# Fused attention and gated MLP on one NeuronCore: where the scale products and the token-mixing bias of two batches are computed, and when eight weight blocks are stored

## The chip, the cores and the metric

One core of a Trainium2 chip runs the whole program. The metric is the device time of one execution in microseconds (us); the time given for a kernel is the median of its runs. The engines are named as the profile names them: PE (TensorE's matmuls), PEld (its weight loads), DVE (VectorE), ACT (ScalarE), POOL (GpSimd) and SP (SyncE, which here only issues DMAs). Each engine executes its own instructions in the order in which the kernel writes them.

## What is computed

Grouped-query attention over 8 batches (16 query heads, 4 key heads, 384 tokens, head size 64) gives `x` of 384 x 1024 per batch. Then comes a block that mixes tokens and channels:

```python
a1 = alpha1 * x + beta1
tok = np.einsum('ts,bsd->btd', w_tok, a1)
u = x + lam * tok
a2 = alpha2 * u + beta2
ch = np.maximum(a2 @ w_ch1, 0.0) @ w_ch2
return (u + lam * ch).astype(np.float32)
```

`w_ch1` is 1024 x 4096, `w_ch2` 4096 x 1024; inputs and output are float32, the products are made in bfloat16.

## The kernel before

**Pairs, phases, steps.** The batches go through the MLP in four pairs (`pair(ps)`, ps = 0 to 3). A pair has phase 0, the product with `w_ch1`, and phase 1, the product with `w_ch2`. Both are made from blocks of the weights in seven products instead of eight, so sums and differences of weight blocks are needed too. `pair` is a generator that yields after every small group of matmuls; each yield is a *step*. In pair 0, phase 0 has 100 steps in eight groups, and phase 1 has 84: 21 turns `(o, ms)` of 16 matmuls, four steps a turn, so turn k ends with step 4k+3. The dictionary `plan` says by hand what is emitted after step (pair, phase, step): `put(0, 1, 41, keep_w2, 1, 0)` emits that call after step 41 of phase 1 of pair 0.

**Attention beside phase 1.** While pair 0 is in phase 1, the attention and token mixing of batches 2 and 3 are emitted between its steps (`side(2)` from step 0, `side(3)` from step 38 on). They go by eight head pairs p:

- `scores3` makes scores on PE, and ACT takes their exponentials (L269);
- `av` (`av_piece`) multiplies by the values on PE (L295); then DVE normalizes (L300, L303) and makes `a1` in bfloat16, the operand of the token mixing;
- `tok` multiplies `a1` by the token weights on PE (L324), DVE adds `x` (L331) and multiplies by alpha2 (L334); SP stores u (`spill`, L227) and, for batch 2, turns a2 by a DMA transpose (L337);
- for batch 3 `turn` turns a2 on PE (L398), and ACT copies it out (L400).

All PSUM tiles of this attention come from `three()`, which hands out three double banks in rotation. `g1` holds alpha1 * lam and `h1` holds beta1 * lam, so that lam * tok comes out of the product directly.

**The fold.** For `fold` batches (0 to 3) `av_piece` makes `a1` with one product (L309), and the bias enters in `tok` by an extra matmul per output block, R against H (L328): R is made of the row sums of the token weights and H of beta1 * lam. H and R lie in the memory of `h1`. Other batches do without that matmul and make `a1` with two DVE operations, a product and an addition (L312, L313). In pair 1, `h1` is filled: `rows4_on` clears two row tiles on POOL and loads beta1 with two SP DMAs, `to_all` spreads it over the partitions on DVE (L1037), `scale_beta` multiplies it by lam on DVE (L1040).

**The second product of pair 0.** `second_product` ends a turn by an ACT copy (L764) and for o = 6 and 7 a DVE addition (L767). Finished output tiles (128 x 512) are queued in `later` and handled by `flush`, which calls `scaled`: a product with lam (L790), on POOL if `lead` (pair 0) and otherwise on DVE, and then an accumulating store (L442), a DMA that POOL issues. In phase 1 of pair 0 nine such tiles are flushed, after the fourth or twelfth matmul of a turn: for steps 12, 16 and 28, and for steps 68, 70, 72, 74, 76 and 78. The last three are flushed in phase 0 of pair 1.

**W2's blocks.** `w_ch2` is cut into blocks "11", "12", "21", "22" with four parts c each. `load_w2` loads them; `sum_w2` overwrites them by sums on DVE (L499). Raw blocks and sums are stored in DRAM tiles `w2s` (`keep_w2`, an SP DMA of 512 KB each), from where later pairs fetch them. Part c of "11" is overwritten by `sum_w2(7, c)` after steps 51, 54, 57 and 58, which has to wait until its store has read it; the slots of "22" are freed by PE in steps 44 to 47. The slots `w` are a ring of six; `pump` gives free ones to the next loads, which POOL issues ("again" blocks: SP).

**Order on the queues.** Instructions of a step are emitted as: matmuls of the step, the end of a turn, a flush, then the plan's entries in the order of their `put`.

Of the kernel before, what the change touches and what calls it, by code (L numbers as in the profile page):

```python
# [13 lines left out]
def kernel(  # L14
# [21 lines left out]
    nc = tc.nc  # L36
# [4 lines left out]
    MUL = mybir.AluOpType.mult  # L41
# [43 lines left out]
    g1, h1, al2, lam_t = (vecs[:, i] for i in range(4))  # L85
# [10 lines left out]
    turn, a2_turn = [0], [0]  # L96
# [117 lines left out]
    def side(b):  # L214
        vb = vt[b % 2]
        ess, avs, a1s, a2s, xr = {}, {}, {}, {}, {}
        first, fold = b < 2, b < 4
        kT_, qT_ = kTs.get(b, kT), qTs.get(b, qT)

        def x_of(p):  # L220
# [170 lines left out]
        def by_pe(p):  # L391
            return b in (0, 3) or b % 2 and p >= NP - (4 if first else 3)
# [14 lines left out]
        def put(k, *m):  # L407
            at.setdefault(k, []).append(m)
# [3 lines left out]
        for p in range(NP):  # L412
            put((4, 10, 14, 18, 24, 29, 33, 35)[p], av, p)
            put((8, 15, 17, 22, 27, 32, 36, 38 if b % 2 else 39)[p], tok_flip, p)
            if by_pe(p):
                put(((13, 20, 22, 28, 34, 37, 40, 42) if b == 3 else (0, 0, 0, 0, 0, 36, 39, 41))[p], turn, p)
        return at

    def loads(b):
# [21 lines left out]
    def store(b, ms, dw, o):  # L441
        nc.gpsimd.dma_start(out=by_tok(out[b])[:, ms, dw * 512:(dw + 1) * 512], in_=o, accum_op=ADD)  # L442
# [19 lines left out]
    def spare(i):  # L462
        at = 24 * S + i % 3 * 1024
        return hTf[:, at:at + 1024]
# [102 lines left out]
    def free_blocks(side, gp):  # L567
        for kind in (side + "1", side + "2"):
            if (kind, gp) in block_slot:
                free(block_slot.pop((kind, gp)))  # L570
# [201 lines left out]
    def pair(i):  # L772
        b0 = 2 * i
        lead = i == 0
# [12 lines left out]

        def scaled(o, b, ms, dw, t):
            if o != 2 or not last:
                (nc.gpsimd if lead else nc.vector).tensor_tensor(out=t, in0=t, in1=lam_t[:, dw * 512:(dw + 1) * 512], op=MUL)  # L790
            store(b, ms, dw, t)

        def flush(n=9):
# [18 lines left out]
        if lead:  # L812
            yield from first_product(flush)
            share_banks("sc0", "acc", "sc1", "sc2")
            yield from second_product(pairs["acc"], later, flush, scaled)
            return

        for g in range(NH // 2):
            X, Y, snap = {}, {}, {}
            for k, (o, e) in enumerate(SEQ1):  # L820
                t = 2 * g + e
# [54 lines left out]
        for k, o in enumerate(PLACE2):  # L876
            whole = not last and o != 4
            tail = last and o == 4
            for h in range(1 if whole else 2):
                for ms in range(NST - (tail and not h)):  # L880
# [37 lines left out]
                    if (whole or h == 1) and not (last and o == 4):  # L918
                        if o in (1, 6, 5):
                            q = ((1, 6, 5).index(o) * NST + ms) * 512  # L920
                            snap[o, ms] = snaps[:, q:q + 512]
                        else:
                            bb, dw = where[o]
                            t = snap[1, ms] if o == 7 else spare(ms).bitcast(f32)
                        for c0, c1, x in X[ms]:
                            if o == 1:
                                nc.scalar.copy(out=snap[o, ms], in_=x)
                            elif o in (6, 5):
                                tt(out=snap[o, ms], in0=x, in1=snap[1 if last or o == 6 else 6, ms], op=ADD)
                            elif o == 2 and last:  # L930
                                tt(out=t, in0=x, in1=lam_t[:, :512], op=MUL)
                            else:
                                base = {2: 1, 3: 1 if last else 5, 7: 5, 4: 6}[o]
                                tt(out=t[:, c0:c1], in0=x, in1=snap[base, ms][:, c0:c1], op=ADD)
                            if o == 7 and not last:
                                tt(out=snap[6, ms], in0=x, in1=snap[6, ms], op=ADD)
                        if o not in (1, 6, 5):
                            later.append((scaled, o, b0 + bb, ms, dw, t))
# [8 lines left out]
    with tc.manual_schedule(engines=order):  # L947
# [123 lines left out]
        def put(ps, phase, at, *m):  # L1071
            plan.setdefault((ps, phase, at), []).append(m)
# [17 lines left out]
        put(0, 0, 8, rows4_on, (3, 0), (3, 1))  # L1090
        put(0, 0, 30, to_all, 3, 0, 0)
        put(0, 0, 34, to_all, 3, 1, 1)
        put(1, 0, 20, rows4_on, (1, 0), (1, 1))
        put(1, 0, 54, to_all, 1, 0, 0)
        put(1, 0, 68, to_all, 1, 1, 1)
        put(1, 0, 62, scale_beta, 0)
        put(1, 0, 76, scale_beta, 1)
        for c in range(4):
            put(0, 0, (50, 72, 74, 44)[c], load_w2, "11", c)
            put(0, 0, (6, 14, 42, 46)[c], cast_w2, "21", c)  # L1100
            put(0, 1, (41, 43, 45, 47)[c], keep_w2, 1, c)
            put(0, 1, 38 + 2 * c, keep_w2, 3, c)
            put(0, 1, (9, 10, 13, 15)[c], sum_w2, 5, c)
            put(0, 1, (20, 21, 25, 26)[c], sums_first_hid, 2, c)
            put(0, 1, (28, 30, 31, 34)[c], sums_first_hid, 4, c)
            put(0, 1, (37, 40, 41, 43)[c], sum_w2, 6, c)
            put(0, 1, (44, 45, 49, 50)[c], sums_first_hid, 3, c)
            put(0, 1, (51, 54, 57, 58)[c], sum_w2, 7, c)
            put(0, 1, (61, 64, 68, 71)[c], last_w2, c)
        for u, o in ((77, 5), (79, 7), (81, 6)):  # L1110
            put(0, 1, u, sum_w1, 0, o)
        for ps in range(NB - 1):
            c = 2 * ps + 2
            for i in range(9):
                put(ps, 0, (4, 8, 12, 16, 20, 24, 54, 58, 62)[i] if ps == 0 else 4 + 7 * i, load_next, c, 1)
                put(ps, 0, 70 + 3 * i if ps == 0 else 91 + 2 * i, load_next, c + 1, 1)
            put_flips(ps, 0, c, (44, 46, 50, 54, 58) if ps == 0 else range(76, 86, 2))
            put_all(ps, 1, side(c))
            for u, f, h in zip((8, 14, 14, 27, 32, 33) if ps == 0 else (10, 17, 18, 28, 33, 33),
                               (flip_q, flip_k, flip_q, flip_q, flip_k, flip_q), (0, 0, 2, 4, 2, 6)):  # L1120
                put(ps, 1, u, f, c + 1, h, 2)
            put_all(ps, 1, side(c + 1), lambda u: u + 38)
            for j, u in ((0, 77), (2, 80), (3, 83)) if ps == 0 else ((0, 76), (2, 79), (3, 81)):
                put(ps, 1, u, sums_a, j, 1 if j else 2)

        def steps(ps):
            done = [0, 0]
            for second in pair(ps):
                for f, *a in plan.pop((ps, second, done[second]), []):
                    f(*a)  # L1130
                done[second] += 1
                yield
            for key in [k for k in plan if k[0] == ps]:
                for f, *a in plan.pop(key):
                    f(*a)

        first = steps(0)
# [76 lines left out]
```

## Time and profile before

| | us |
|---|---|
| runs of the kernel | 732.49, 732.74, 738.95 (median 732.74) |
| profiled execution, its own time | 731.92 |
| its span, first to last instruction | 729.9 |
| pair 0, phase 0 | about 59 to 129 |
| pair 0, phase 1 (with batches 2 and 3) | about 129 to 234 |
| pairs 1 to 3 | about 234 to 725 |

The profile is of one execution; its own time is 2.0 us longer than its span. A row of groups has the source line, the engine, the operation, output and input, the shape and count, then the busy time in us and the mean of one in ns, then idle time before it. A row of the timeline has the start, the duration, the engine, the line and the instruction, and in brackets the idle time of the engine before it and what ended that.

### The profile page before, as it was taken

Reading aid. Unit: us, or ns where it says so; the run is one execution under the profiler, and the core shown is the slowest. Engines: PE = TensorE matmul, PEld = TensorE weight load, DVE = VectorE, ACT = ScalarE, POOL = GpSimd, SP = SyncE. Lnnn points to the kernel's source line nnn. Section 1 sums busy time; section 2 is a strip of 40 time slices with the busy share of each in tenths; the row PEclk is TensorE's granted clock in tenths of the full one; section 3 lists DMA queues with packets and bytes.
Section 4 is the critical chain, followed back from the end, with each engine's and each line's share of the span. In section 5 each row is a group of like instructions: output and inputs, shape, how many; then the busy total and the mean of one; then the engine's idle time right before and its main releaser. Section 6 shows DMA issues by size and latency. Waiting matters only on the chain.

```text
span 729.9 us, 14511 instructions
## 1 busy us (share of the span) xinstructions
PE 717.4 (98%) x5716; PEld 408.7 (56%) x5716; DVE 543.9 (75%) x1009; ACT 373.8 (51%) x566; POOL 199.2 (27%) x242
## 2 busy tenths in 40 slices
PE   8899999999999999999999999999999999999998
PEld 4665555555555666555555566655555566654444
DVE  7888876577888988649678888748868988763354
ACT  7877666544563666643433466663333366650000
POOL 8844233221046551201022344200002222000011
PEclk9999999999999999999999999999999999999999
DMA  9999999999999999969989999998989999937965
GB/s 164 180 239 231 190 195 227 226 242 235 366 312 232 179 182 196 234 221 207 272 193 220 160 162 194 212 227 201 270 233 183 210 126 146 165 123 264 302 174 104
DMA packets 197616, 153.26 MB, mean 210 GB/s; under 512 B 90540, under 2 KB 175892, under 8 KB 197292
## 3 DMA queue, kind: packets, MB, share of 16 engines
q0 software_dynamic: 109872, 64.47, 65.4%
q1 hardware_dynamic: 86988, 87.42, 42.8%
q8 instruction: 44, 0.72, 0.4%
q10 hardware_dynamic: 688, 0.46, 0.2%
q14 instruction: 24, 0.20, 0.1%
HBM read 155.23 MB, written 39.85 MB: 267 GB/s over the span
## 4 chain that ended last, share of the span: by engine, by line
PE 90%; DVE 4%; POOL 2%; DMA 1%; issue 1%; ACT 1%; DVEq 0%; ACTq 0%; POOLq 0%
PE C L897 30%; PE X L831 17%; PE C L752 10%; PE Y L831 9%; PE Z L831 4%; PE sc L260 4%; PE X L681 4%; PE sc L295 3%; PE sc L324 3%; PE Y L681 3%; DMA ops<-obuf 1%; DVE pad L565 1%; PE Z L681 1%; PE tok L324 1%; POOL obuf L334 0%
## 5 line engine op out<-in xcount | busy, mean ns | idle before, releaser
L897 PE MATMUL C<-w,arena 128*128 128x512 bf16 (+2 forms) x744 | 168.3, 372 | 0.0
L269 ACT ACTIVATE es<-sc 128x1024 bf16<-128x1024 f32 x108 | 104.1, 1024 | 116.0 <-PE sc L260 107.6
L897 PEld LDWEIGHTS <-arena 128*128 128x128 bf16 x1040 | 94.8, 98 | 100.5 <-issue 5.1
L442 POOL DMA_DIRECT2D out_dram<-hT x45 | 40.0, 888 | 294.7 <-DVE hT L790 135.9
L836 ACT ACTIVATE hT<-X,bias 128x384 f32<-128x384 f32 x144 | 83.6, 582 | 60.0 <-PE X L831 55.2
L831 PEld LDWEIGHTS <-w 128*128 128x128 bf16 x768 | 75.1, 98 | 50.0
L831 PEld LDWEIGHTS <-pad 128*128 128x128 bf16 x576 | 56.4, 98 | 37.2
L183 POOL DMA_DIRECT2D w<-in_moe_w_ch_dram x48 | 45.4, 1002 | 105.6 <-PE X L831 36.5
L831 PE MATMUL X<-ops,w 128*128 128x384 bf16 x384 | 70.3, 326 | 0.0
L831 PE MATMUL X<-ops,pad 128*128 128x384 bf16 x384 | 70.3, 326 | 0.0
L897 PE MATMUL C<-pad,arena 128*128 128x512 bf16 (+2 forms) x296 | 70.2, 373 | 0.0
L324 PEld LDWEIGHTS <-wtokT 128*128 128x128 bf16 x576 | 39.0, 98 | 16.4 <-issue 3.4
L752 PEld LDWEIGHTS <-arena 128*128 128x128 bf16 x336 | 29.8, 98 | 30.0 <-issue 2.5
L331 DVE TENSOR_TENSOR xr<-sc,xr 128x384 f32<-128x384 f32 x48 | 26.5, 553 | 25.6 <-PE sc L324 14.3
L752 PE MATMUL C<-w,arena 128*128 128x512 bf16 x168 | 41.2, 379 | 0.0
L838 DVE TENSOR_TENSOR arena<-Y,hT 128x384 bf16<-128x384 f32 x48 | 26.5, 556 | 17.7 <-ACT hT L836 16.0
L295 PEld LDWEIGHTS <-es 128*128 128x128 bf16 x864 | 32.8, 97 | 11.3
L831 PE MATMUL Y<-ops,w 128*128 128x384 bf16 x192 | 39.1, 326 | 0.0
L831 PE MATMUL Z<-ops,w 128*128 128x384 bf16 x192 | 39.0, 326 | 0.0
L269 ACT ACTIVATE hT<-sc 128x1024 bf16<-128x1024 f32 x36 | 35.8, 1031 | 4.3 <-PE sc L260 4.0
L260 PE MATMUL sc<-qT,kT 64*128 64x384 bf16 (+2 forms) x504 | 37.2, 271 | 0.5 <-ACT hT L269 0.2
L842 ACT ACTIVATE arena<-X,bias 128x384 bf16<-128x384 f32 x48 | 27.9, 582 | 17.7 <-PE X L831 16.1
(190 smaller groups left out, 1175.1 us busy)
## 6 DMA issues: line engine op xcount, KB each, us to landing
w<-w2s SPq DMA_DIRECT2D x67, 512.0 KB, 5.1
w<-in_moe_w_ch_dram POOLq DMA_DIRECT2D x65, 512.0 KB, 9.8
pad<-w2s SPq DMA_DIRECT2D x25, 512.0 KB, 6.9
out_dram<-hT POOLq DMA_DIRECT2D x45, 256.0 KB, 7.1
out_dram<-xr SPq DMA_DIRECT2D x48, 192.0 KB, 5.3
q_raw<-in_q_dram POOLq DMA_DIRECT2D x28, 192.0 KB, 9.5
w2s<-w SPq DMA_DIRECT2D x10, 512.0 KB, 7.6
arena<-in_moe_w_ch_dram POOLq DMA_DIRECT2D x8, 512.0 KB, 15.9
```

Of the source, the lines that this page charges most:

```text
L183: nc.gpsimd.dma_start(out=w1[:, w1_slots[c]], in_=w1src[:, :, c * CW * P:(c + 1) * CW * P])
L260: nc.tensor.matmul(out=sc[:, hh, k % 4:k % 4 + n], lhsT=kT_[r, 2 * p // G, BLK[hh][sk], :], rhs=qT_[r, p, st:st + n, :], start=True, stop= ...
L269: nc.scalar.activation(out=e, in_=sc, func=EXP, scale=scale_qk)
L295: nc.tensor.matmul(out=av[:, hh, sq, :], lhsT=ess[k // 4][:, m % 2, k % 4, :], rhs=vb[:, sk, hk, :], start=(sk == 0), stop=(sk == NST - 1))
L324: nc.tensor.matmul(out=ps[:, tt, :], lhsT=wtokT[:, st, tt * P:(tt + 1) * P], rhs=a1s[p][:, st, :], start=(st == 0), stop=(st == NST - 1 an ...
L442: nc.gpsimd.dma_start(out=by_tok(out[b])[:, ms, dw * 512:(dw + 1) * 512], in_=o, accum_op=ADD)
L681: nc.tensor.matmul(out=ps[:, :n], lhsT=tb[G, o][:, dt, e * P:(e + 1) * P], rhs=opb(FIRST1[o], n)[:, dt], start=(o in (1, 2, 7) and dt == 0 ...
L752: nc.tensor.matmul(out=x, lhsT=lead_hid[:, t, FIRST2[o], ms * P:(ms + 1) * P], rhs=rhs[:, t % 4 * 512:(t % 4 + 1) * 512], start=(o in (1, ...
L831: nc.tensor.matmul(out=ps, lhsT=tb[g, o][:, dt, e * P:(e + 1) * P], rhs=opb(LEFT1[o])[:, dt], start=(o in (1, 2, 7) and dt == 0), stop=(dt ...
L836: nc.scalar.activation(out=snap[o, e], in_=ps, func=IDENT, bias=hi if o == 5 else lo)
L842: nc.scalar.activation(out=hid[:, t, 4], in_=ps, func=RELU, bias=hi)
L897: nc.tensor.matmul(out=x, lhsT=hid[:, t, LEFT2[o], ms * P:(ms + 1) * P], rhs=rhs[:, t % 4 * 512 + c0:t % 4 * 512 + c1], start=((not last o ...
```

## The change

Four things are edited, all in what pair 0 does or in what batches 2 and 3 do.

1. Batches 2 and 3 are no longer folded: no L328 matmuls, and `a1` by L312 and L313.
2. For that, `h1` has to be filled before batches 2 and 3: `rows4_on`, `to_all` and `scale_beta` move from phase 0 of pair 1 to phase 0 of pair 0 (steps 40, 54, 59, 64 and 69), when batches 0 and 1 are done with H and R.
3. The lam products of pair 0 go to DVE; POOL still issues the stores.
4. The stores of the raw "11" and "22" go from steps 38 to 47 to steps 16 to 37. Besides, `turn` of p = 2 of batch 3 is emitted one step later (step 61 instead of 60, behind `tok` of p = 3).

```diff
-        first, fold = b < 2, b < 4
+        first = fold = b < 2
...
-                put(((13, 20, 22, 28, 34, 37, 40, 42) if b == 3 else (0, 0, 0, 0, 0, 36, 39, 41))[p], turn, p)
+                put(((13, 20, 23, 28, 34, 37, 40, 42) if b == 3 else (0, 0, 0, 0, 0, 36, 39, 41))[p], turn, p)
...
-                (nc.gpsimd if lead else nc.vector).tensor_tensor(out=t, in0=t, in1=lam_t[:, dw * 512:(dw + 1) * 512], op=MUL)
+                nc.vector.tensor_tensor(out=t, in0=t, in1=lam_t[:, dw * 512:(dw + 1) * 512], op=MUL)
...
-        put(1, 0, 20, rows4_on, (1, 0), (1, 1))
-        put(1, 0, 54, to_all, 1, 0, 0)
-        put(1, 0, 68, to_all, 1, 1, 1)
-        put(1, 0, 62, scale_beta, 0)
-        put(1, 0, 76, scale_beta, 1)
+        put(0, 0, 40, rows4_on, (1, 0), (1, 1))
+        for i in range(2):
+            put(0, 0, 54 + 10 * i, to_all, 1, i, i)
+            put(0, 0, 59 + 10 * i, scale_beta, i)
...
-            put(0, 1, (41, 43, 45, 47)[c], keep_w2, 1, c)
-            put(0, 1, 38 + 2 * c, keep_w2, 3, c)
+            put(0, 1, (16, 18, 20, 22)[c], keep_w2, 1, c)
+            put(0, 1, (24, 32, 34, 37)[c], keep_w2, 3, c)
```

## Prediction

> **What bounds the kernel now.** I read the busy shares first, then the chain of work that ended last, then the stage that is changed in the stretches table, and last the timelines of PE, DVE, POOL and SP there.
>
> ```profile
> PE 717.4 (98%) x5716; PEld 408.7 (56%) x5716; DVE 543.9 (75%) x1009; ACT 373.8 (51%) x566; POOL 199.2 (27%) x242
> ...
> PE 90%; DVE 4%; POOL 2%; DMA 1%; issue 1%; ACT 1%; DVEq 0%; ACTq 0%; POOLq 0%
> ```
>
> PE is busy nearly throughout, at a granted clock of 1.00, and carries 90% of the chain. From 234.5 to 725 the stretches show PE busy without a gap, so whatever pair 0 gains or loses arrives at the end. The change acts in 77 to 235 us. Its stretches (length, then busy time of PE, PEld, DVE, ACT, POOL):
>
> ```profile
> 190.00:200.00 10.00, 10.00 (x106) 5.84 (x105) 8.43 (x13) 5.29 (x8) 0.91 (x1) 1.00 1.00 359
> 200.00:212.00 12.00, 11.41 (x107) 6.29 (x106) 9.95 (x15) 7.33 (x12) 0.96 (x2) 1.00 1.15 333
> 212.00:220.00 8.00, 8.00 (x91) 4.68 (x88) 6.86 (x9) 5.31 (x9) 7.08 (x7) 1.00 1.25 273
> 220.00:228.00 8.00, 6.81 (x72) 4.03 (x69) 7.57 (x10) 3.58 (x7) 7.03 (x7) 1.00 1.17 240
> 228.00:235.00 7.00, 7.00 (x41) 3.47 (x39) 6.86 (x16) 1.97 (x4) 1.60 (x2) 1.00 1.05 240
> ```
>
> PE rests twice: near 204, and between 220 and 228, where DVE is full. The chain in 190 to 236 names the two places (start, duration, what):
>
> ```profile
> 203.81 1.04 ACT es L269
> 204.85 0.04 issue
> 204.89 0.33 PE sc L324 x3
> ...
> 220.87 2.02 DVE w L499
> 222.89 0.11 DVE rinv L300
> 223.00 0.02 issue
> 223.03 0.57 DVE xr L303
> 223.60 0.02 issue
> 223.62 1.09 DVE a L309
> 224.71 0.04 issue
> 224.76 0.34 PE sc L324 x3
> ```
>
> At 204.89 `tok` of p = 3 waits for a PSUM bank that the second exponential releases; at 224.76 `tok` of p = 6 waits for its `a1`. Two durations in that second chain are too long: L499 of this shape takes 1.22 elsewhere, L309 0.56. Both run beside POOL's lam products:
>
> ```profile
> L790 POOL TENSOR_TENSOR hT<-hT,vecs 128x512 f32<-128x512 f32 x12 | 18.6, 1552 | 17.6 <-ACT hT L764 17.6
> L790 DVE TENSOR_TENSOR hT<-hT,vecs 128x512 f32<-128x512 f32 x30 | 20.6, 686 | 0.4
> L309 DVE TENSOR_TENSOR a<-xr,vecs 128x384 bf16<-128x384 f32 x16 | 11.8, 736 | 0.6
> L312 DVE TENSOR_TENSOR a1f<-xr,vecs 128x384 f32<-128x384 f32 x32 | 17.9, 558 | 1.1
> ```
>
> L309 averages 736 ns where the like L312 averages 558. The long ones start while a POOL product runs (L309 at 143.15 takes 1.33, POOL's product lasts from 142.79 to 144.05).
>
> **The change part by part.**
>
> *48 matmuls less.* The chain shows one L328 as 0.06 us, and three L324 as 0.17; 48 x 0.0557 = 2.67 us of PE, in a stage where PE has work. I take -2.67.
>
> *`turn` of p = 2 behind `tok` of p = 3.* In 203.87 to 204.89 the turn takes the bank that the first exponential frees (done at 203.81) and `tok` waits for the second (204.85). With the order changed, `tok` can start at 203.9, and the turn follows four matmuls later, when its bank is free. PE's rest there, from 204.14 to 204.89, goes: -0.75. The next limit is `a1` of p = 3, which by the ledger below is ready 0.3 us ahead.
>
> *DVE in phase 1.* Added: 16 more `a1` operations, 0.585 from start to start (L303 at 223.03, L309 at 223.62, same shape): 9.4 us. Nine lam products, 0.61 each from start to start (L767 of that shape): 5.5 us. Removed: the stretching beside POOL. Adding the excess of each long operation over its usual time gives 0.77 + 0.49 before 150 us, and 1.21 + 0.37 + 0.80 + 0.52 + 1.18 = 4.1 after 212; together 5.3. Removed too is a wait of 1.1 at 203 to 204.1, where L499 wants a W2 part whose store has not read it; the stores go out some 25 steps sooner. Up to 190 us, DVE's idle gaps (about 1 us in front of most `av`) take up the additions. From 192 on there are few. A ledger of DVE's order from the addition L767 that ends turn k = 12 (193.61 before, about 192.1 after) to `a1` of p = 6: before, 31.1 us, of which 3.1 idle and 2.9 stretched, so 25.1 of work; after, 25.1 + 5 x 0.585 + 2 x 0.61 = 29.2, which ends at 221.4. PE would want it at 223.65 less 2.5 (15 pieces of 0.167) less 0.75 and less small waits ahead of it: 220.5. So the rest of about 1.1 us at `tok` of p = 6 stays at about 0.9, and p = 7 waits 0.1: I take -0.1, between -1.1 (no rest) and +3.7 (below). At the end of the phase DVE closes at about 233.2 with the last sums of the operands, which the third product of pair 1 needs at 233.6: 0.4 us to spare. L515 and L510, next on DVE, have 2.9 us idle in 235 to 238.
>
> *POOL.* Without products it only issues stores (0.9 us each) and comes sooner to its weight loads. Nobody on PE waits for those: 0.
>
> *Phase 0: `to_all` and `scale_beta`, 4 operations, 2.8 us of DVE.* Each group there has DVE idle for 1.8 to 2.2 us in front of L693. Those for steps 59 and 64 fall into that gap: 0. Step 54 comes behind L698 and step 69 behind L565, ahead of L702, whose read frees the Y bank for the next group's third product. There L702 ends at 101.05 and PE takes the bank at 101.40: of 0.62 us, 0.3 is left over, twice: +0.6, between 0 and +1.3.
>
> *Phase 0: `rows4_on`.* Two SP loads of 8 KB ahead of SP's transposes at 77.8, whose results are used after 129: 0. Two memsets on POOL, behind the load at 77.16, so in 77.9 to 79.0. There DVE runs L565, L561, L565 and L698 without a gap, and PE waits 0.45 for that L698 at 79.94. The only memsets beside a DVE operation of two-port kind are in pair 1:
>
> ```profile
> 245.21 1.04 POOL L1087 MEMSET rows<- 128x512 f32 x2
> ...
> 244.57 1.90 DVE L861 TENSOR_SCALAR arena<-arena 128x768 bf16<-128x768 bf16 x1
> ```
>
> L861 takes 0.36 when alone and here outlasts both memsets. The memsets of step 8, beside L702 (67.29, 2 x 0.61), stretched nothing. L565 is like neither: between 0 and +1.0, I take +0.5. The Trainium skill (GPSIMD Engine Reference, Key points) says that GpSimd shares its SBUF interfaces with VectorE and contends with VectorE instructions in a two-port mode or with two SBUF inputs. By that rule L565, with two SBUF inputs, is held, and the sum below would be 0.5 higher; if memsets hold only two-port operations it would be 0.5 lower.
>
> *Pair 1, phase 0* loses those operations (2.8 us of DVE) and does three lam products on DVE (2.1). PE has no gap there: 0.
>
> *The stores.* SP is full from 178.7 to 198 before (about 20 issues) and has pauses between 158 and 178, so SP gains order. "11" has long landed at step 16. "22" parts 1 to 3 are loaded by POOL from 158.5 on; median landing 9.6, so 168 to 171, about when steps 32 to 37 come (168 to 178). If SP has to wait there, behind it stand a spill, the a2 transposes of batch 2 (used in pair 1) and the q and k transposes of batch 3, used in 202: 25 us of cover. I take 0, between 0 and +3 (rival 2).
>
> **Sum.** -2.67 - 0.75 - 0.1 + 0.6 + 0.5 = -2.4. From the profiled execution's own 731.92 (its span 729.9 and 2.0 around it) that gives 729.5. The median of the runs, 732.74, is 0.8 above that execution; -2.4 from there is 730.3. I say 729.9.
>
> **The rivals.**
>
> 1. *DVE becomes the bound (slower than before).* In 190 to 235 DVE was busy 39.7 of 45 us. If the stretching stays, because POOL's store issues or the loads it now reaches sooner hold DVE as the products did, the 4.1 us are not given back: DVE ends 4.1 later, 0.4 of that is spare, and PE waits 3.7 more, at `tok` of p = 6 and 7 and at the third product of pair 1. -2.4 + 3.7 = +1.3: 733.6 with the median as base. It decides against the change when DVE loses 2.8 us or more. Against it: L499 at 144.40 takes 1.21, its usual time, right beside a store issue (144.37, 0.95). For it: the ledger is tight, and each us of error counts whole. Half of it gives 731.8.
>
> 2. *The stores delay the loads of "22".* Five more stores, 2.6 MB, enter 150 to 178. That stretch moves 210 GB/s, 180 to 200 moves 368, so there is room, but behind all of them a load would be 7 us later. PE wants part 1 at 173.1 (174.3 before); 4 to 5 us are spare. PE would wait about 3 us: -2.4 + 3 = +0.6, 732.9. The Trainium skill (DMA: Bandwidth & Descriptors, Queues, rings and completion order) says that each DMA engine takes turns between the queue rows, packet by packet. By that rule SP's stores would slow POOL's loads rather than stand in front of them; no row here separates the two.
>
> 3. *The shorter PE work is only replaced by waits.* If PE keeps DVE's present pace from 212 on (the chain there is DVE's), the matmuls saved in that part and the bank wait bring nothing: 2.67 x 10/16 = -1.7, + 1.1 for phase 0: -0.6, 731.7. For it: DVE 6.86 of 7 in 228 to 235. Against: the stretching there is what made DVE late.
>
> **How the numbers follow.** Forecast (728 to 731) 0.62, rival 1 0.17, rival 2 0.08, rival 3 0.13. The low end has all costs at their best: -2.67 - 0.75 - 1.1 = -4.5, from 731.9: 727.4. The high end is that of rivals 1 and 2: 733.4. A change of less than 1% (7.3 us) is about what a measurement of this kernel can't tell from none. No case reaches -7.3, leaving 0.02 for faster; slower by over 7.3 needs rival 1 and 2 at twice their price: 0.05; within 1%: 0.93.
>
> **What would show it.** Right: no L328 of form sc; `tok` of p = 3 with no rest ahead; L309 gone and L312 x48 at 0.56; L499 never 2 us; PE's last gap, about 0.9, still ahead of `tok` of p = 6; pair 1 starting about 2.4 sooner (231.5 to 232.5); in phase 0 two waits of 0.3 on L702 and one longer at 79.9. Wrong: L790 on DVE well above 0.69, PE waits on L331 or on a bank after 205, a wait on a W2 load near 173, or DVE's sums later than pair 1's third product.

## The result, and the profile after

The changed kernel takes 740.78 us (median of 7 runs, 738.63 to 746.16), the kernel before 732.74 beside it (7 runs, 732.49 to 738.95): a ratio of 1.0109, with a 95% interval of 1.0083 to 1.0135. Here and below, medians are over all runs of a kernel, and the ratios and intervals leave out its slow runs, those over 1.5% above its fastest, so a ratio need not be the quotient of two medians. The profiled execution of the changed kernel took 740.78, its span is 739.0 (729.9 before). The prediction was 729.9, in a range of 727.4 to 733.4: wrong in sign and outside the range.

The busy shares and the chain of waits of the kernel after, on its page, in the same order as those shown of before:

```profile
PE 719.1 (97%) x5668; PEld 407.0 (55%) x5668; DVE 550.3 (74%) x1037; ACT 373.6 (51%) x566; POOL 181.0 (24%) x230
...
PE 74%; DMA 11%; issue 6%; DVE 4%; POOL 4%; ACT 1%; POOLq 0%; ACTq 0%; DVEq 0%
```

PE has 48 matmuls less and is busy 1.7 us longer. That can't be work: PE ran part of it at a lower clock (the rows of the clock are shown further on). In the chain, DMA has gone from 1% to 11%, and PE from 90% to 74%. That share says which way the chain was followed back and not how long PE waited: 36.7 us of it are two transfers of v in 92 to 132 (24.81 and 11.93), beside which PE waits 0.42 us up to 130. What PE waited for, over the whole span (in total, times, longest):

```profile
PE X L831 <- DVE ops L850: 4.0, 1, 4.0
PE C L752 <- DMA w<-in_moe_w_ch_dram: 3.5, 1, 3.5
...
PE Y L831 <- DVE arena L844: 0.9, 1, 0.9
PE sc L324 <- DVE a L313: 0.7, 1, 0.7
...
PE Y L681 <- DVE arena L702: 0.4, 2, 0.2
```

The lines of L850, L752 and L844 don't occur in the kernel before; they come to 8.4 us. The stretches say where they lie (length, then busy time of PE, PEld, DVE, ACT, POOL, then the granted clock, DMA share and GB/s):

```profile
170.00:180.00 10.00, 6.46 (x60) 3.53 (x59) 6.48 (x11) 4.58 (x6) 0.00 (x0) 0.93 1.18 244
...
190.00:200.00 10.00, 10.00 (x98) 5.45 (x96) 8.02 (x14) 6.22 (x10) 0.90 (x1) 1.00 1.02 251
200.00:212.00 12.00, 11.99 (x112) 6.39 (x110) 11.73 (x20) 6.58 (x10) 0.00 (x0) 1.00 1.05 375
212.00:220.00 8.00, 8.00 (x79) 4.42 (x79) 7.05 (x13) 6.07 (x9) 1.75 (x2) 1.00 1.06 235
220.00:228.00 8.00, 7.04 (x80) 4.20 (x78) 7.79 (x15) 3.28 (x5) 2.36 (x3) 1.00 1.16 230
228.00:235.00 7.00, 7.00 (x47) 3.61 (x46) 6.86 (x14) 3.00 (x6) 1.94 (x3) 1.00 1.00 195
235.00:250.00 15.00, 10.97 (x56) 5.72 (x54) 8.02 (x18) 5.85 (x10) 5.18 (x6) 0.90 1.15 156
```

The rest near 204 is gone (11.99 of 12.00, 11.41 before), the one in 220 to 228 is a little shorter (7.04, 6.81 before). Two new holes stand beside the region that the prediction looked at: 3.5 us in 170 to 180 and 4.0 us in 235 to 250. The chain through the first (start, duration, what):

```profile
159.29 0.73 POOL w L491
160.03 0.08 issue
160.11 0.01 POOLq L442
160.12 19.23 DMA w<-in_moe_w_ch_dram
179.36 0.04 issue
179.40 1.86 PE C L752 x4
181.26 0.96 PE sc L324 x9
```

A load of "22", issued by POOL, takes 19.23 us to land; before, the slowest of the three took 12.8, with PE never waiting for one. The landing of the three, before and after:

```profile
DMA to landing us min/median/max: 5.8/9.6/12.8
...
DMA to landing us min/median/max: 11.9/13.9/19.2
```

Call this wait A. The chain through the second, wait B:

```profile
232.40 2.94 issue
235.33 0.04 POOLq L183
235.38 0.54 POOL out_dram L442
235.91 8.75 DMA w<-in_moe_w_ch_dram
244.66 0.02 issue
244.69 0.70 DVE pad L515
245.39 0.04 DVEq L510
245.42 0.83 DVE ops L850
246.26 0.05 issue
246.30 2.16 PE X L831 x8
```

Read it from the end. PE's next product of pair 1 waits for the sum L850; that stands on DVE behind L515, which waits for a W1 load; that load was issued at 235.91, because it stood on POOL behind the last accumulating store L442; and that store waited for its lam product. POOL's timeline of the kernel after shows the order (start, duration, what, idle before and its releaser):

```profile
231.55 0.84 POOL L442 DMA_DIRECT2D out_dram<-hT  x1 [0.58 <-DVE hT L790]
235.35 0.84 POOL L442 DMA_DIRECT2D out_dram<-hT  x1 [2.95 <-DVE hT L790]
235.91 2.98 POOL L183 DMA_DIRECT2D w<-in_moe_w_ch_dram  x3
```

and that of before, in the same place:

```profile
227.05 0.87 POOL L442 DMA_DIRECT2D out_dram<-hT  x1 [0.30 <-POOL hT L790]
232.10 0.92 POOL L183 DMA_DIRECT2D w<-in_moe_w_ch_dram  x1 [4.17 <-PE sc L398]
234.32 1.80 POOL L183 DMA_DIRECT2D w<-in_moe_w_ch_dram  x2 [1.30 <-PE C L752]
```

On POOL a product needed its operand and no more, and the last store left at 227.05. On DVE the last product stands in order behind the sums L448 to L450:

```profile
232.84 0.55 DVE L448 TENSOR_TENSOR ops<-ops 128x768 bf16<-128x768 bf16 x1
233.42 0.56 DVE L449 TENSOR_TENSOR ops<-ops 128x768 bf16<-128x768 bf16 x1
233.90 0.55 DVE L450 TENSOR_TENSOR ops<-ops 128x768 bf16<-128x768 bf16 x1
234.37 0.68 DVE L790 TENSOR_TENSOR hT<-hT,vecs 128x512 f32<-128x512 f32 x1
```

So the last store leaves 8.3 us later, and three W1 loads behind it go out together at 235.91, where one had gone at 232.10 and two at 234.32.

**The account.** Landmarks are the Y product behind the wait for L698 (79.94 before, 79.26 after; phase 0 has then run for some 20 us), the last Y product of phase 0 (126.77, 126.83; phase 1 begins 1.3 us later), and the first product of pair 1 (234.38, 235.94). "Phase 0" and "phase 1" in this table and below are measured between them:

| stretch | before | after | difference |
|---|---|---|---|
| up to that Y product | 79.94 | 79.26 | -0.7 |
| phase 0 | 46.83 | 47.57 | +0.7 |
| phase 1 | 107.61 | 109.11 | +1.5 |
| pair 1 to the end of the span | 495.5 | 503.1 | +7.5 |

The first row isn't the change's: it lies ahead of it but for the memsets at its end, the wait of 0.45 on L698 is the same in both, and in the experiments below it varies between 79.3 and 82.3 without order (86.9 in e6, which waits 6.4 us near its start), so single spans can differ by some 3 us for it. Phase 1 holds wait A; the last row holds wait B and the wait of 0.9 on L844.

### The profile page after: what moved, and what is told of

The parts are those of the page before. It is cut to its first block, busy times and chain, and to the rows that moved or that the text cites. A ratio compares the mean times of both kernels' runs of the same rounds, so it can differ in the third digit from the quotient of the medians.

```text
span 739.0 us, 14413 instructions
## 1 busy us (share of the span) xinstructions
PE 719.1 (97%) x5668; PEld 407.0 (55%) x5668; DVE 550.3 (74%) x1037; ACT 373.6 (51%) x566; POOL 181.0 (24%) x230
## 4 chain that ended last, share of the span: by engine, by line
PE 74%; DMA 11%; issue 6%; DVE 4%; POOL 4%; ACT 1%; POOLq 0%; ACTq 0%; DVEq 0%
PE C L897 30%; PE X L831 14%; PE Y L831 7%; DMA w<-in_moe_w_ch_dram 6%; DMA v<-in_v_dram 5%; PE Z L831 4%; PE sc L260 4%; PE C L752 4%; PE sc L295 3%; PE sc L324 3%; PE X L681 2%; PE E L613 1%; PE Y L681 1%; PE tok L324 1%; PE av L295 1%
## 5 line engine op out<-in xcount | busy, mean ns | idle before, releaser
L442 POOL DMA_DIRECT2D out_dram<-hT x45 | 39.3, 873 | 346.4 <-DVE hT L790 184.6
L831 PEld LDWEIGHTS <-w 128*128 128x128 bf16 x768 | 75.4, 98 | 55.9 <-DVE ops L850 4.4
L831 PEld LDWEIGHTS <-pad 128*128 128x128 bf16 x576 | 56.6, 98 | 38.1 <-issue 1.2
L831 PE MATMUL X<-ops,w 128*128 128x384 bf16 x384 | 70.9, 328 | 4.0 <-DVE ops L850 4.0
L831 PE MATMUL X<-ops,pad 128*128 128x384 bf16 x384 | 70.2, 326 | 0.0
L752 PEld LDWEIGHTS <-arena 128*128 128x128 bf16 x336 | 30.0, 98 | 33.6 <-issue 6.6
L752 PE MATMUL C<-w,arena 128*128 128x512 bf16 x168 | 42.0, 385 | 3.5 <-DMA w<-in_moe_w_ch_dram 3.5
L838 DVE TENSOR_TENSOR arena<-Y,hT 128x384 bf16<-128x384 f32 x48 | 26.5, 557 | 18.3 <-ACT hT L836 16.4
L831 PE MATMUL Y<-ops,w 128*128 128x384 bf16 x192 | 39.2, 326 | 0.9 <-DVE arena L844 0.9
L831 PE MATMUL Z<-ops,w 128*128 128x384 bf16 x192 | 39.7, 330 | 0.0
```

The source lines that it names most:

```text
L752: nc.tensor.matmul(out=x, lhsT=lead_hid[:, t, FIRST2[o], ms * P:(ms + 1) * P], rhs=rhs[:, t % 4 * 512:(t % 4 + 1) * 512], start=(o in (1, ...
L831: nc.tensor.matmul(out=ps, lhsT=tb[g, o][:, dt, e * P:(e + 1) * P], rhs=opb(LEFT1[o])[:, dt], start=(o in (1, 2, 7) and dt == 0), stop=(dt ...
```

## The experiments

The theory: two causes that add up. A: the early stores run beside the loads of "22", which so land late. B: the products on DVE end late, POOL issues in order, and the W1 loads behind the last stores come late. Rivals: DVE's added work itself is the bound (rival 1 of the prediction), or A and B are one. Times are medians; "ratio" is against the kernel before on the same chip.

**1. Three parts put back, one at a time (changes to the kernel after).** The stores back at their old steps:

```
-            put(0, 1, (16, 18, 20, 22)[c], keep_w2, 1, c)
-            put(0, 1, (24, 32, 34, 37)[c], keep_w2, 3, c)
+            put(0, 1, (41, 43, 45, 47)[c], keep_w2, 1, c)
+            put(0, 1, 38 + 2 * c, keep_w2, 3, c)
```

> The changed kernel with the eight stores put back to steps 38 to 47; products still on DVE. Theory: two separate late loads make the changed kernel slow, and the stores make the first (PE waits 3.5 us near 176 for a part of 22, then runs some matmuls at half the clock, 4.9 us in all). Without the early stores that goes and the wait in pair 1 near 242 to 246 stays: 740.8 - 4.9 = about 736, with the three parts of 22 landed by 172. Rival (the 16 additional a1 operations and the products overload DVE, which holds everything up): the stores' place doesn't matter, about 740 and PE still rests near 176.

Measured: 737.87, ratio 1.0074 (1.0053 to 1.0094). Wait A is gone, wait B is 4.8 us (4.0 with the stores early). Phase 1 is 104.64 us, 2.97 shorter than before: without A, the change does as a whole nearly what was predicted there (3.5).

The lam products back on POOL, the stores early:

```
-                nc.vector.tensor_tensor(out=t, in0=t, in1=lam_t[...], op=MUL)
+                (nc.gpsimd if lead else nc.vector).tensor_tensor(out=t, in0=t, in1=lam_t[...], op=MUL)
```

> The changed kernel with the lam products of pair 0 back on POOL; stores still early. Theory: the wait of 4.0 us in pair 1 comes from POOL's queue: its last store waits for DVE's product (234.4), and the W1 loads stand behind it (235.9 instead of 232.1 to 234.3). With POOL's own products the loads go out near 232 again, and pair 1's first group has no wait: 740.8 - 6.2 - 0.9 = about 734, or up to 735 as DVE is stretched again; the wait near 176 stays. Rival (SP's stores and the other traffic delay the W1 loads): the loads land late again and the wait in pair 1 stays, about 740.

Measured: 738.34, ratio 1.0078 (1.0048 to 1.0107). The mechanism is as expected, the time isn't (734 to 735). Wait B is gone, A is 2.0 us. In their place PE waits 4.3 us for L313 (3.1 at 222.68): the now more numerous `a1` operations are stretched beside POOL's products, L312 and L313 to 2.46 us each instead of 0.56 (217.67 and 220.17, POOL's L790 from 218.12 and 220.64).

Both put back, so that only the `a1` operations of batches 2 and 3 and the moved steps of phase 0 are left:

> The changed kernel with both put back: only the matmuls of the fold away, two a1 operations, beta1 filled in phase 0 and the turn one step later. Theory: neither wait is there and PE's saving is kept: 732.7 - 2.67 - 0.75 + 0.74 = about 730 to 731, L309 gone and L312 at 0.56 to 0.75. Rival (the additional DVE work itself costs more than the matmuls save): 733 to 737, with waits of PE for a1 or for a bank.

Measured: 736.24, ratio 1.0070 (1.0038 to 1.0101). This missed: I expected the gain of the saved matmuls. PE waits 5.1 us for L313 (4.3 in one place). DVE in 226 to 229 of this run:

```profile
226.18 2.44 DVE L313 TENSOR_TENSOR a<-a1f,vecs 128x384 bf16<-128x384 f32 x1
```

POOL's L790 runs beside it, from 226.63 to 228.19. So the part of the change that saves PE work loses time by itself, as long as the products are on POOL. The two moves of work to DVE and off POOL belong together, and wait B is the price of the second.

**2. Each cause alone on the kernel before.** Only the eight early stores:

> The kernel before with nothing but the eight stores moved to the early steps. Theory: the wait near 176 for a part of 22 comes with it, 3.5 to 5 us: 736 to 738. Rival (the loads of 22 are late because of what POOL and DVE do in the changed kernel): the stores alone cost nothing or save up to 1 us (DVE's wait of 1.1 near 203): 732 to 733.

Measured: 735.38, ratio 1.0043 (1.0021 to 1.0066), with a wait of 3.0 us on a load of "22" that took 19.2. The time is a little under the 736 to 738 expected. The stores alone make A.

Only the products on DVE:

> The kernel before with nothing but the lam products of pair 0 on DVE. Theory: DVE loses the stretching beside POOL (so PE's wait of about 1 us for a1 near 224 gets shorter), but the last three stores leave POOL only after DVE's products, and the W1 loads behind them land later; how much PE then waits in pair 1's first group depends on the last product: before about 229.5 no wait, later a wait of 2 to 5 us. 731.5 to 736. Rival (the late W1 loads come only from DVE's overload by the unfolded a1): no wait in pair 1, at most 732.5.

Measured: 738.58, ratio 1.0061 (1.0024 to 1.0097), PE waits 4.1 us for L850 with the last L442 at 232.94 and three W1 loads together at 233.51. The time is above the 731.5 to 736 expected, the wait as expected for a late product. The products alone make B; the `a1` operations aren't needed for it.

**3. Wait B taken away.** The stores late as in e1, and the products allowed into the order two turns sooner:

```
-                    if t % 8 == 3 and later and (later[0][1] == 1 or k > 16 and later[0][1] != 4):
+                    if t % 8 == 3 and later and (later[0][1] == 1 or k > 14 and later[0][1] != 4):
```

> The run with late stores (products on DVE, unfolded) with one more edit: the last six tiles are flushed from turn 15 on instead of 17, so that the last product is emitted after step 72 instead of 78. Theory: POOL's last store is gone by 227 to 229, the W1 loads issue near 229 to 231 as their slots come free, and PE's wait of 4.8 us in pair 1 goes, with its slow matmuls 6 to 7 us: 737.9 - 6 = about 732. PE may wait up to 1 us more for a1 near 215 to 222. Rival (the loads are slow for another reason): the wait in pair 1 stays, 737 to 738.

Measured: 733.42 (10 runs), ratio 1.0018 (0.9981 to 1.0055), 4.5 us less than e1. The last L442 goes out at 226.60, the W1 loads at 232.84 and 235.07 as before, and PE's wait for L850 is 0.7. That the wait went with the place of the products in DVE's order, with the same work on every engine, shows B's cause. A wait of 1.9 us is left at 211.68: DVE, which PE waits for there, has lost 1.29 at 205.71, where L499 waits for a store of "11", and has no gap after that.

The same with the `a1` part taken out (the kernel before, products on DVE, queued sooner):

> The kernel before with products on DVE and the last six tiles flushed from turn 15 on; fold, stores and turn as before. Theory (the products on DVE cost only by the stores that hold up POOL's W1 loads): no wait in pair 1, and DVE, without the stretching and without the unfolded a1, is in time for a1 near 224: about 1 us under before, 731 to 732. Rival (products on DVE cost DVE more than the stretching did): 733 or more with a wait for a1 or a bank. Beside the unfolded kernel with the same flush (733.4) it also says whether unfolding pays: if this one is faster, it doesn't.

Measured: 733.87 (12 runs), ratio 1.0007 (0.9981 to 1.0033): the same as e8 within the intervals, and above the 731 to 732 expected; PE still waits 1.0 us for L850. Its phase 1 is 106.67 us, that of e8 106.55. So what the saved matmuls give can't be told from nothing here; section 5 says where part of it goes.

**4. Which stores make A.** On the kernel before, "11" early alone and "22" early alone, one execution each:

> The kernel before with only the four stores of 11 early (steps 16 to 22), those of 22 late. Theory: these four go out right ahead of POOL's three loads of 22 and share the DMA engines with them; a part of 22 lands 18 us after its issue and PE waits 2 to 3 us near 178: 735. Rival (the stores of 22, which wait for those loads on SP, are what delays): no wait, 732.

> The kernel before with only the four stores of 22 early (steps 24 to 37). Theory: only part 0 goes out ahead of the loads, the other three can't leave before the loads land; the loads land as before, no wait near 178: 732. Rival: a wait of 2 to 3 us near 178, 735.

Measured: "11" alone has a wait of 2.1 us on a load of "22" (741.46, but with an unrelated wait of 6.4 us at its start). "22" alone (738.29) has none; in its place SP comes up to 5 us later to the stores of "11", DVE's L499 waits 3.43 for one of them, and PE waits 2.0 and 0.8 us in 209 to 212. A single execution doesn't settle the split, so I made the same choices again with B removed:

> The changed kernel without the wait in pair 1, stores of "22" back where they were, stores of "11" at steps 33 to 37, behind the landing of the loads of "22". Theory (a store costs nothing where no load is in flight beside it): no PE wait near 178, and the wait of 1.9 us near 211 that late stores of "11" leave goes too: 731 to 732. Rival (any sooner store costs): the stores keep SP from the transposes, or "22" is late all the same, with a wait of 2 to 4 us in 170 to 215: 734 or more.

> The changed kernel with only the flush sooner: all eight stores stay early. Theory (two causes that add up): the wait in pair 1 goes (under 1.5 us instead of 4.0), the wait near 176 on the load of "22" stays (3 to 4 us with a slow load of some 19 us): 737 to 738, near half of the change's loss. Rival (the causes are one): the wait near 176 goes as well, or the one in pair 1 comes back, 734 or 740.

> The changed kernel without the wait in pair 1, only the stores of "11" early (steps 16 to 22). Theory (stores beside the loads of "22" are what delays them): a PE wait of 2 to 4 us near 176 for a load of "22" that takes 16 us or more, 736 to 738. Rival (it takes the stores of "22" too): no such wait, 733 to 734.

> The changed kernel without the wait in pair 1, only the stores of "22" early (steps 24 to 37). Theory: the loads of "22" land in time, so no PE wait near 176; but SP comes later to the stores of "11" than in the kernel before, DVE's L499 waits for them, and PE waits 2 to 3 us in 205 to 215: 735 to 737. Rival (stores of "22" by themselves delay the loads): a wait near 176.

Measured, with e8 as the base (landing is that of the slowest load of "22"; GB/s of 150 to 180):

| early stores | time | ratio, interval | landing | GB/s | PE's wait for it | phase 1 |
|---|---|---|---|---|---|---|
| none (e8) | 733.42 | 1.0018 (0.9981 to 1.0055) | 13.3 | 229 | 0 | 106.55 |
| "11" at 33 to 37 (e12) | 732.64 | 0.9999 (0.9970 to 1.0028) | 13.4 | 255 | 0 | 105.18 |
| "11" at 16 to 22 (e14) | 734.34 | 1.0012 (0.9992 to 1.0032) | 17.0 | 255 | 1.3 | 106.50 |
| "22" at 24 to 37 (e15) | 737.26 | 1.0058 (1.0038 to 1.0078) | 14.9 | 258 | 0 | 110.40 |
| all eight (e13) | 735.69 | 1.0045 (1.0016 to 1.0074) | 19.1 | 280 | 3.4 | 108.60 |

Both sets of stores delay the loads, "11" by 3.7 us and "22" by 1.6; together it is 5.8, and PE has some 15.7 of cover (17.0 - 1.3, and 19.1 - 3.4). The landing repeats from trace to trace: 12.2 to 13.4 in the nine kernels with no early store ahead of the loads (before, e1, e3, e5, e8, e9, e11, e12, e16), 17.0 and 18.3 with "11" early (e14, e6), 14.9 and 15.1 with "22" early (e15, e7), 17.7 to 19.2 with all eight (after, e2, e4, e13); e10, below, stands apart. The bytes per second of the stretch don't say it: e12 and e14 move the same 255, but in e12 "11" goes out behind the loads, and they land in 13.4. In 160 to 175, when the loads are under way, the two differ, 234 and 270 GB/s. That the stores delay the loads by sharing the DMA engines with them is argued from this and not shown: early stores also push SP's transposes back beside the loads (one of q from 165.46 to 170.19 in the kernel after). "22" early alone costs the most, and by another way: no PE wait on its loads, but SP is late for "11" (as in e7), L499 waits 1.60, 1.18 and 1.85, and PE rests 2.8 us in all on L303 and 2.0 on L499. In e13 the stores of "11" go first, so only A is seen. And A and B add up within the intervals: after less e13 is 5.1 us, after less e1 is 2.9, together 8.0, and after less e8 is 7.4.

e14 falls below what I expected (736 to 738): its wait is 1.3, not 2 to 4, and its interval holds 1. e13 is below its 737 to 738, with the wait as expected, and e12 and e15 are just above their 731 to 732 and 735 to 737.

The other way to have "11" early is ahead of the loads of "22", in steps 4 to 7 (on the kernel before):

> The kernel before with only the four stores of 11 moved, to steps 4 to 7 (134 to 139 us), where POOL has no load under way. Theory: sooner is not the trouble, but what they run beside; these are done before POOL loads 22 at 158, so no wait near 178, and DVE's wait of 1.1 us for a store near 203 goes: 731.5 to 732.5. Rival (any store ahead of the loads delays them or SP's transposes): a wait of 2 to 3 us near 178, 735.

Measured: 737.98, ratio 1.0050 (1.0015 to 1.0085). This missed, and its rival came true. The trace is of the slowest of the nine executions (745.51). In it the stores go out at 126 to 128, not at 134 to 139, beside the loads of "12"; DVE's L499 waits for those, three times in 139 to 147 (3.6 us in all), and PE rests 2.6 at 145. Then the loads of "22", issued at 162 to 164, take up to 22.0 us, and PE waits 3.3 and 1.4 us for them at 182 and 186, though the early stores went out 34 us ahead of them: beside them is one store of a block (out at 158.08), with SP's a2 transposes and stores of u. So more than the early stores can make these loads late. What the other eight executions waited for, no trace shows.

The one PE change alone, `turn` of p = 2 behind `tok` of p = 3 (on the kernel before):

> The kernel before with only the turn of p = 2 one step later. Theory: PE's rest of 0.6 to 0.75 near 204 goes, but tok of p = 6 near 224 waits for DVE, which is not sooner, so that part of it comes back there: 731.9 to 732.6. Rival (it pays whole): 731.8; (it costs, as the turn then holds a bank at a worse place): 733.

Measured: 733.55, ratio 1.0004 (0.9970 to 1.0038). The rest near 204 is gone as predicted, but `tok` of p = 6, where `a1` sets the time, waits 1.7 in place of 0.9, and a bank another 0.7 (L303): given back within 20 us.

**5. Where the rest of the gain went.** In e12 phase 1 is 2.43 us shorter than before, phase 0 is 0.75 longer, and the time is that of before. DVE at the start of pair 1 in e12:

```profile
240.56 0.69 DVE L515 TENSOR_TENSOR pad<-w 128x1024 bf16<-128x1024 bf16 x1 [5.03 <-DMA w<-in_moe_w_ch_dram]
```

The two loads ahead of it went out at 234.50, 0.06 before pair 1's first product, exactly as in the kernel before (234.32 and 234.38). But they reach DVE after 6.1 us where it was 3.8, and PE waits 1.6. The same line in the kernel before:

```profile
238.07 0.69 DVE L515 TENSOR_TENSOR pad<-w 128x1024 bf16<-128x1024 bf16 x1 [2.92 <-DMA w<-in_moe_w_ch_dram]
```

In 224 to 244, e12 moves 4.66 MB and the kernel before 4.23, with the DMA engines busy nearly throughout: I take it that the shorter phase 1 leaves less time for the same transfers. To see whether the bytes set it, I left out the last two stores of xr there, so this kernel's output is not complete:

```
         def spill(p):
+            if b == 3 and p >= 6:
+                return
```

> The version with "11" behind the loads and the wait in pair 1 removed, without the last two stores of xr of phase 1 (L227 for batch 3, p = 6 and 7, 2 x 192 KB, issued at 228; that part of the output is left out). Theory (the DMA engines are full ahead of pair 1, so that a phase 1 that is 2.4 us shorter makes PE wait for W1 in its place): 0.39 MB less at some 200 GB/s are 1.9 us less to move, so the load that DVE's L515 waits for lands 1 to 2 us sooner, PE's wait of 1.6 us falls under 0.5, and the time is 731 to 732. Rival (the load takes its time whatever runs beside it): the wait stays at 1.3 to 1.7 us, 732.6.

Measured: 731.87, ratio 0.9989 (0.9957 to 1.0020). The loads, out at 231.96, are there 3.9 us later:

```profile
235.85 0.69 DVE L517 TENSOR_TENSOR pad<-w 128x1024 bf16<-128x1024 bf16 x1 [2.85 <-DMA w<-in_moe_w_ch_dram]
```

and PE's wait is gone (L517 is L515, two lines on). So in e12 the transfers into pair 1 set its first group, just behind PE. How much shorter phase 1 may be before that happens isn't shown: in e8, e14 and e9 it is 0.9 to 1.1 us shorter and PE waits 0.7, 1.4 and 1.0 for L850, but in e11, where it is 1.4 longer, PE waits 0.5. By the medians the difference between e12 and e16, 0.8 us, lies within the intervals; one trace of each carries this reading. No kernel that computes everything beat the one before measurably; e12 equals it.

## Why the prediction was wrong

Point by point, in the order of its sum.

*48 matmuls less, and the turn: -2.67 - 0.75 - 0.1.* Right in place, and near in size only as a whole. No L328 of form sc is left, `tok` of p = 3 has no rest in front, `tok` of p = 6 waits 0.7 as foreseen. Phase 1 without wait A is 2.97 shorter (e1) or 2.43 (e12), against 3.5. But the products on DVE, which this part of the sum gave no gain, shorten it by 1.13 alone (e5: 106.48, after 107.61), and the unfolding with the turn only by another 1.84 (from e5 to e1), where the sum has 2.67 + 0.75. That the whole came out near was in part luck. The turn alone on the kernel before (e11) gives nothing.

*DVE in phase 1.* Right. Groups of the kernel after:

```profile
L790 DVE TENSOR_TENSOR hT<-hT,vecs 128x512 f32<-128x512 f32 x42 | 28.8, 685 | 0.7 <-ACT hT L764 0.4
...
L312 DVE TENSOR_TENSOR a1f<-xr,vecs 128x384 f32<-128x384 f32 x48 | 26.8, 558 | 1.7
```

L312 stays at 558 ns and no L499 takes 2 us: the stretching came from POOL's products and left with them. e2 and e3 show the other side of that, 2.4 us for an operation of 0.56. So rival 1 (store issues and loads stretch DVE too) didn't happen.

*Phase 0: +0.6 and +0.5.* The first was right: two waits of 0.22 and 0.20 on L702, and phase 0 is 0.74 longer (the other 0.3 is in no wait that the trace names). The second was wrong: the memsets ran from 78.17 to 79.17, and the operation beside them was not held. DVE in the kernel after:

```profile
77.99 0.69 DVE L565 TENSOR_TENSOR pad<-w,pad 128x1024 bf16<-128x1024 bf16 x1
```

It takes 0.69, as the same operation before (78.67), and the two L698 behind it take 1.14 in both kernels, so this term was 0. The rule of the Trainium skill that the prediction weighed (GPSIMD Engine Reference, Key points: contention with VectorE instructions of two SBUF inputs) doesn't show for memsets here; beside POOL's products of two SBUF inputs it does (L313 2.44 instead of 0.56).

*The step that failed first: "Without products it only issues stores (0.9 us each) and comes sooner to its weight loads. Nobody on PE waits for those: 0."* The reverse happened. I asked what POOL no longer had to do, and not what its stores now had to wait for. The product was the operation ahead of each store, on the same engine. Once it is on DVE, the store waits for DVE's order, and everything behind that store on POOL waits too. I had even written that DVE closes at 233.2 with 0.4 us to spare, and that L515 had 2.9 us idle; the load that L515 waits for was one queue further on. Cost: the first group of pair 1 takes 15.30 us instead of 9.10, +6.2. Y's wait of 0.9 near 281, behind a W1 load that was issued at 260.18 (as early as before) and took 15.2 us, isn't shown to be B's: e15 and e13 have it too (0.9 and 0.6), without B.

*The second: "The stores. [...] I take 0, between 0 and +3 (rival 2)."* Rival 2 described what happened, in the right place (a wait on a W2 load near 173; it ended at 179.40), with 3 us (it was 3.54), but at a chance of 0.08. It said that behind all five stores a load would be 7 us later; it was 6.4 (19.2 against 12.8). Its cover of 4 to 5 us was too large: 15.7 less 12.8 is 2.9. I took 0 because 210 GB/s left room up to the 368 seen later. The average rate of 30 us doesn't bound what a load waits for within 15.

*What no price held: the clock after a rest.* The granted clock of the kernel after, three stretches:

```profile
176.00:179.00 3.00, 0.00 (x0) 0.00 (x0) 0.69 (x1) 2.32 (x3) 0.00 (x0) 0.95 1.13 242
179.00:182.00 3.00, 2.60 (x13) 1.49 (x13) 0.00 (x0) 0.67 (x2) 0.00 (x0) 0.50 1.36 219
248.00:252.00 4.00, 4.00 (x19) 2.13 (x18) 3.02 (x6) 1.31 (x2) 2.85 (x4) 0.71 0.94 105
```

After the rest of 3.54 the clock is 0.50, and four L752 take 1.86 us, after the rest of 3.99 eight L831 take 2.16 instead of 1.46. PE in e13, after a rest of 3.37:

```profile
181.65 1.02 PE L752 MATMUL C<-w,arena 128*128 128x512 bf16 x3 [3.37 <-DMA w<-in_moe_w_ch_dram]
```

Those are at full speed (no L752 there takes over 0.39 us, where one in the kernel after takes 0.63), and the clock is 1.00, as it is after the rest of 3.03 in e4. So that wait of 3.4 us cost itself, and the two of 3.5 and 4.0 cost 1.4 and 2.2 us more: this is how 3.5 + 4.0 became 4.9 + 6.2. The Trainium skill (TensorE: Matmul & The Clock Gate, Part 1) states an idle window of about 3.4 us behind which the clock falls to half. The five rests of 3.5 us and more behind 130 us in these traces agree (3.54 and 3.99 here, 4.76 in e1, 4.31 in e3, 4.05 in e5: each is followed by 0.50), and so do e4 and e13. Some shorter ones don't. In e2, the clock falls to 0.50 within 4 us after rests of 2.00 and of 3.14, and twelve L752 behind the first take 4.5 us instead of 2.9; in e7, after a rest of 1.96 (and one of 0.86 five us ahead of it), it is 0.50 as well, and eight L752 take 3.57 instead of 1.89. After rests of 1.91 in e8 and e15 it stays at 1.00. What decides there stays open; the length of one rest alone does not.

*The sum.* By the table of the account: -0.7 (not the change's) + 0.74 + 1.5 (+4.9 for A, an estimate from the wait of 3.54 and the slow matmuls behind it, and -3.4 as what is left) + 7.5 (6.2 for B, 0.9 for Y's wait, 0.4 not assigned) = +9.1 in the span of the profiled execution; the medians differ by 8.0. The gain side of the prediction was right to 1 us as a whole, though not term by term, and both losses came from queues beside the stage that it worked out. The range had a slip besides: its high end was to be that of rivals 1 and 2, but rival 1's +1.3 on the median of 732.74 is 734.0, not 733.6 or 733.4. No case in it comes near 740.8.

## What to carry to other kernels

When an operation moves to another engine, list what stood behind it on the old one: a DMA that needs its result is now released by the new engine's order, and every load behind that DMA in the same in-order queue comes late with it. When stores are moved sooner, look at which loads are under way in that same window and how much cover each has (how long it may take before an engine waits), not at the average rate of the stage. And test the parts of a change both alone and together: here one part lost time until another removed the contention, and the gain of two parts was taken back by transfers that were just hidden before.

## What was not expected of the hardware

DVE operations beside products on POOL were stretched by more than before: L313 took 2.44 and L312 2.46 us in e3 and e2, against 0.56, where the kernel before had 1.74 at most for the like L309. The slowest of three loads of 512 KB took 19.2 us with eight stores of another queue put early, and 17.0 with four of them, where it took 12.8 before; in e10 it took 22.0, with the early stores long gone. The clock stayed at 1.00 after a rest of 3.37 us and fell to 0.50 after one of 3.54, but after 1.96 (e7), 2.00 and 3.14 (e2) too.
